# Attention and SoLU on one core: moving squares, row sums, additions and a weight combination within a quad

## The chip, the core and the metric

The kernel runs on one core of a Trainium2 chip. The metric is the device time of one execution, in microseconds (us), and lower is better. Five engines work side by side, each through its own queue in order: TensorE (PE; its weight loads are shown as PEld), VectorE (DVE), ScalarE (ACT), GpSimd (POOL) and SyncE (SP), which here issues nearly all DMAs. They meet through semaphores.

## The reference

```python
def _attn_ref(q, k, v, g_q, g_k):            # q, k, v: (8, 12, 448, 64)
    def rmsnorm(x, g):
        rms = np.sqrt(np.mean(x * x, axis=-1, keepdims=True) + 1e-06)
        return x / rms * g
    q_n, k_n = (rmsnorm(q, g_q), rmsnorm(k, g_k))
    scores = 1.0 / np.sqrt(q.shape[-1]) * np.matmul(q_n, k_n.transpose(0, 1, 3, 2))
    scores = scores - np.max(scores, axis=-1, keepdims=True)
    attn = np.exp(scores)
    attn = attn / (np.sum(attn, axis=-1, keepdims=True) + 1e-09)
    return np.matmul(attn, v).astype(np.float32)

def _moe_ref(x, w_in, w_out, g_ln):          # x: (3584, 768), w_in: (768, 1024), w_out: (1024, 768)
    h = x @ w_in
    e = np.exp(h - np.max(h, axis=-1, keepdims=True))
    sm = e / (np.sum(e, axis=-1, keepdims=True) + 1e-09)
    solu = h * sm
    mu = np.mean(solu, axis=-1, keepdims=True)
    var = np.mean((solu - mu) ** 2, axis=-1, keepdims=True)
    ln = (solu - mu) / np.sqrt(var + 1e-06) * g_ln
    return (ln @ w_out).astype(np.float32)
```

The output of the attention, reordered to (batch x sequence, heads x 64), is the x of the second part. The weights come as 64-bit floats.

## The kernel before

`fast_path` has two stages. The attention stage works on *pairs* of heads, numbered n, and on *quads* m of two pairs a = 2m and b = 2m + 1: 24 quads. The second stage, which starts when the last quad is done, multiplies by w_in and w_out in blocks of two by two with seven products each (`products`, matmuls on L953). The diff changes the attention stage alone; a slower `general_path` is compiled too and does not run here.

The order of all work in the attention stage is written out by hand (`tc.manual_schedule`): each engine runs its instructions in the order in which the Python loop over m calls the functions. `unit(f)` calls f and then what was put off with `later`.

For a pair n the steps are:

- `load(n)` (L610): eight DMAs on SyncE's queue bring q and k into `qk`. Quad m issues those of pairs 2m + 6 and 2m + 7, two of them used a quad later.
- `squares(n)` (L632): ScalarE squares `qk` into `sq`. `row_sums(n)` (L640): VectorE sums blocks of 32 into `part`. Quad m does this for quad m + 2. `fold_sums(m + 2)` (L650, L651): GpSimd joins the halves of a row of both pairs into `ss` by four copies and one addition.
- at the top of quad m, for quad m + 1: `rsqrt_seed` (L670, L671; two ScalarE instructions, into `ny`), `rsqrt_step` (L677 to L680; VectorE), and two times `normalise` (L689; GpSimd, into `qkn`).
- `qk_transpose(n)` (L699): VectorE transposes `qkn` into `qkT`; `gain(n)` (L703): ScalarE scales the half that belongs to q.
- `scores` and `scores_last` (L771, L784): TensorE, into three PSUM buffers `s`; `exponentials` (L761): ScalarE, seven a quad, into `E`.
- `add(n)` (L798): VectorE adds two tiles of E into `es`, so that `sums` (L843) needs fewer matmuls for the row sums of the softmax. In the last two quads `add_more` (L803) adds a third.
- `values_last`, `values` (L813, L824) and `sums` on TensorE; `inverse` (L854, L855 on VectorE, L862 on GpSimd) and, a unit later, `divide` (L869, L870; into `xo`), and `store_x` (L875; SyncE, to DRAM).

Beside this, the weights are turned into 32-bit floats: `load_w` brings one piece a quad into `raw` (L503 for w_in, L508 for w_out), and `convert_w` yields `low_bits` (L525, L526; ScalarE), `join` (L531, L532; VectorE) and, for w_out, `product` (L537; ScalarE), which run in three quads in turn. From quad 12 on, `combine(w_in, ...)` (L552) subtracts one block of w_in from another on GpSimd, one block a quad; quads 22 and 23 also combine two blocks of w_out. At the end of quad 22 `load_x` and `sizes` (L893, L902) begin to bring the second stage's input.

Buffers that matter here: `qk` has 4, `sq` 1, `raw` 2, and the tag `x` of the pool `xs`, 4, which the first two pairs use at the start and the second stage later.

Of the kernel before, what the change touches and what calls it, by code (L numbers as in the profile page):

```python
# [9 lines left out]
FP32 = mybir.dt.float32  # L10
U32 = mybir.dt.uint32
# [355 lines left out]
def fast_path(  # L367
# [26 lines left out]
    DM, DFF = moe_w_in.shape  # L394
# [97 lines left out]
    def load_w(step):  # L492
        src, c, i = step
        n = HO if src is moe_w_out else DFF // 2
        if second is None:
            raw = work.tile([P, DFF // 2, 2], U32, tag="raw", name="raw", bufs=2)[:, 0:n]
        else:

            raw = second.tile([P, S, 2], U32, tag="again", name="raw", bufs=2)[:, 0:n]
        w = src.bitcast(U32)[:, 2 * i * n : 2 * (i + 1) * n]  # L500
        to = raw.rearrange("p n t -> p (n t)")
        if src is moe_w_in:
            nc.sync.dma_start(to, w[c * P : (c + 1) * P])  # L503
        else:

            for g in range(4):
                r = ((c // HF * 4 + g) * HF + c % HF) * 32
                nc.sync.dma_start(to[g * 32 : g * 32 + 32], w[r : r + 32])  # L508
        return raw
# [37 lines left out]
    def combine(w, x):  # L547

        c, i = divmod(x, 4)
        b11, b21, b22, t1, t3, t2, t4 = [w[:, k, c] for k in range(7)]  # L550
        o, p, q = [(t3, b22, t1), (t1, t1, b11), (t2, b22, t1), (t4, b21, t2)][i]
        nc.gpsimd.tensor_tensor(o, p, q, OP.subtract)  # L552
# [50 lines left out]
    def load(n):  # L603
        b, hp = divmod(n, NP)
        h0 = 2 * hp
        d = st[n] = {}
        d["qk"] = loads.tile([P, 2, NB, 32], FP32, tag="qk", name="qk", bufs=4)
        for s, src in enumerate((q, k)):
            for g in range(4):
                nc.sync.dma_start(  # L610
                    d["qk"][g * 32 : g * 32 + 32, s],
                    src[b, h0 + g // 2].rearrange("(b t) (x d) -> x t b d", t=32, x=2)[g % 2],
                )
# [14 lines left out]

    def squares(n):
        d = st[n]  # L630
        d["sq"] = work.tile([P, 2 * NB, 32], FP32, tag="sq", name="sq", bufs=1)
        nc.scalar.activation(d["sq"], d["qk"].rearrange("p s b d -> p (s b) d"), AF.Square)  # L632


# [1 line left out]
    def row_sums(n):  # L636
        m, i = divmod(n, 2)
        if i == 0:
            norms[m] = {"part": small.tile([P, 2, 2 * NB], FP32, tag="part", name="part", bufs=2)}
        nc.vector.tensor_reduce(norms[m]["part"][:, i], st[n]["sq"], AX, OP.add)  # L640
# [41 lines left out]
    def normalise(n, e=nc.gpsimd):  # L682
        d = st[n]
        if ("one", n) in norms:
            y = norms["one", n]["y"]
        else:
            y = norms[n // 2]["y"][:, n % 2 * 2 * NB : (n % 2 + 1) * 2 * NB]
        d["qkn"] = work.tile([P, 2 * NB, 32], FP32, tag="qkn", name="qkn", bufs=2)
        e.tensor_tensor(  # L689
            d["qkn"],  # L690
            d["qk"].rearrange("p s b d -> p (s b) d"),
            y.rearrange("p b -> p b ()").to_broadcast([P, 2 * NB, 32]),
            OP.mult,
        )

    def qk_transpose(n):
        d = st[n]
        d["qkT"] = work.tile([P, 2, S], FP32, tag="qkT", name="qkT", bufs=3)
        nc.vector.transpose(d["qkT"].rearrange("p s t -> p (s t)"), d["qkn"].rearrange("p b d -> p (b d)"))  # L699
# [95 lines left out]
    def add(n):  # L795
        d = st[n]
        d["es"] = work.tile([P, 2, S], FP32, tag="es", name="es")
        nc.vector.tensor_tensor(d["es"], d["E", 0], d["E", 1], OP.add)  # L798
# [350 lines left out]
    with tc.manual_schedule():  # L1149
# [19 lines left out]
        for m in range(NQ):  # L1169
            a, b = 2 * m, 2 * m + 1  # L1170

            def outputs():
                values_last(m)
                values(a)


            next1 = m + 1 < NQ
            next2 = m + 2 < NQ
            next3 = m + 3 < NQ
            if m == 0:  # L1180
                unit(lambda: scores(a, 0))
                normalise_rows(1, 0)
                normalise_rows(1, 1)
                unit(lambda: scores(a, 1))
                for s in range(2):
                    transpose_rows(1, s)
                    take_rows(1, s)
                squares(2)
                row_sums(2)
                unit(lambda: scores(a, 2))  # L1190
                fold_one(2)
                unit(lambda: scores_last(m))
                rsqrt_seed(norms["one", 2])
                rsqrt_step(norms["one", 2])
                normalise(2)
                add(a)
                unit(lambda: scores(b, 0))
                unit(lambda: scores(b, 1))
                unit(lambda: scores(b, 2))
                squares(3)  # L1200
                row_sums(3)
                qk_transpose(2)
                fold_one(3)
                gain(2)
                rsqrt_seed(norms["one", 3])
                add(b)
                rsqrt_step(norms["one", 3])
                normalise(3)
                load_v(1)
                load(6)  # L1210
                load(7)
                for _ in range(2):
                    load_next()
                unit(outputs)
                squares(4)
                row_sums(4)
                unit(lambda: values(b))
                squares(5)
                unit(lambda: sums(m))
                inverse(m)  # L1220
                qk_transpose(3)
                row_sums(5)
                fold_sums(2)
                later(1, lambda m=m: divide(m))
                continue
            early = 1 < m and next1
            if early:
                rsqrt_seed(norms[m + 1])
                rsqrt_step(norms[m + 1])
                normalise(a + 2)  # L1230
                normalise(b + 2)
            if next1:
                load_v(m + 1)
            unit(lambda: scores(a, 0))
            store_x(m - 1)
            if early:
                qk_transpose(a + 2)
                if next3:
                    load(a + 6)
            unit(lambda: scores(a, 1))  # L1240
            if m == 1:
                gain(b)
            unit(lambda: scores(a, 2))
            unit(lambda: scores_last(m))
            add(a)
            unit(lambda: scores(b, 0))
            if m == 1:
                rsqrt_seed(norms[m + 1])
                rsqrt_step(norms[m + 1])
                normalise(a + 2)  # L1250
                normalise(b + 2)
                load(a + 6)
                load(b + 6)
            unit(lambda: scores(b, 1))
            if early:
                qk_transpose(b + 2)
                if next3:
                    load(b + 6)
            if m >= NQ // 2:
                combine(w_in, m - NQ // 2)  # L1260
            if m >= NQ - 2:
                for i in range(2):
                    combine(w_out, 2 * (m - NQ + 2) + i)
            unit(lambda: scores(b, 2))
            if m == 1:
                qk_transpose(a + 2)
            if next2:
                squares(a + 4)
                row_sums(a + 4)
            if next1:  # L1270
                gain(a + 2)
            add(b)
            if m == 1:
                qk_transpose(b + 2)
            if next1 and m > 1:
                gain(b + 2)
            if next2:
                squares(b + 4)
            if m == 1:
                gain(b + 2)  # L1280
            if next2:
                row_sums(b + 4)
                fold_sums(m + 2)
            add_more(a)
            add_more(b)
            unit(outputs)
            step(m - 2)
            begin(m)
            step(m - 1)
            if m - 1 in sets:  # L1290
                load_next()
            unit(lambda: values(b))
            if m == NQ - 1:
                block_sums(0, "A", 0)
                block_sums(0, "A", 1)
                load_x(1)
            unit(lambda: sums(m))
            inverse(m)
            if next1:
                later(1, lambda m=m: divide(m))  # L1300
            if m == NQ - 2:
                load_x(0)
                sizes(0)
# [105 lines left out]
```

## Time and profile before

| | |
|---|---|
| median of three runs | 852.91 us (852.55 to 857.69) |
| the profiled execution | 855.39 us, of which the profile's span is 853.6 us |
| granted TensorE clock, mean | 0.998 |
| PE, DVE, ACT, POOL busy in the span | 830.1, 616.3, 375.9, 323.1 us |
| attention stage | up to 342.3 us of the span |
| squares L632 (ACT), 46 | 972 ns each |
| row sums L640 (DVE), 46 | 1074 ns each |
| fold's copies L650 (POOL), 88 | 374 ns each |
| normalisations L689 (POOL), 46 | 1713 ns each |
| transposes L699 (DVE), 46 | 1101 ns each |
| additions L798 (DVE), 48 | 1350 ns each |
| combinations of w_in L552 (POOL), 12 | 1271 ns each |

The span runs from the first to the last instruction of the profiled execution; all positions in it are counted from its start. A row of the timeline has a start, a length, the engine, the line, the operation, what is written and read, and a count where like instructions are merged; a bracket at its end tells how long the engine had been idle and what ended that. "SPq" rows are SyncE issuing DMAs. A matmul's end is modelled, so that a busy TensorE may still be waiting; the distance between the same instruction of two quads is the better measure.

### The profile page before, as it was taken

The page shows a single profiled execution, that of the slowest core. Times are in us where ns is not written, and L with a number is a line of the kernel's source. Part 1 is how long each engine was busy: PE and PEld are TensorE (multiplying, and loading weights), DVE is VectorE, ACT ScalarE, POOL GpSimd, SP SyncE. Part 2 cuts the span into 40 slices and gives each one's busy share as a digit, 9 for nine tenths or more (in the row PEclk, how much of TensorE's full clock was granted, in tenths as well). Part 3 has the DMA queues.
Part 4 walks back from the last instruction along what each step waited for, and adds up shares of the span by engine and source line. Part 5 has one row for each costly group of instructions (what it writes and reads, how often), then busy time and mean ns, then how long its engine had stood idle before and what let it go on. Part 6 is the DMA issues. An engine that isn't in the chain of part 4 may idle for free.

```text
span 853.6 us, 13057 instructions
## 1 busy us (share of the span) xinstructions
PE 830.1 (97%) x4432; PEld 481.6 (56%) x4432; DVE 616.3 (72%) x990; ACT 375.9 (44%) x559; POOL 323.1 (38%) x464
## 2 busy tenths in 40 slices
PE   5999999999999999999999999999999999999997
PEld 2334434333433333444444444445999999999996
DVE  5778988799998889589999999999933333333322
ACT  5677877778787776155445453443200000000000
POOL 1444443546455457222333223554333222233220
PEclk9999999999999999999999999999999999999999
DMA  5677777888767673234443444453564445544331
GB/s 119 138 173 177 171 178 156 181 188 172 175 146 174 135 188 118 73 97 132 109 124 105 128 113 105 135 137 92 153 227 151 151 151 182 179 151 141 119 117 41
DMA packets 268060, 121.63 MB, mean 142 GB/s; under 512 B 190672, under 2 KB 250064, under 8 KB 267984
## 3 DMA queue, kind: packets, MB, share of 16 engines
q1 hardware_dynamic: 253584, 110.65, 50.4%
q10 hardware_dynamic: 14400, 10.06, 4.1%
q8 instruction: 37, 0.61, 0.3%
q14 instruction: 39, 0.32, 0.1%
HBM read 83.96 MB, written 36.70 MB: 141 GB/s over the span
## 4 chain that ended last, share of the span: by engine, by line
PE 67%; DVE 11%; SPq 7%; DMA 7%; ACT 3%; issue 2%; POOL 2%; ACTq 0%; POOLq 0%; DVEq 0%
PE b L953 59%; SPq L610 7%; DVE es L798 3%; PE o L824 3%; PE s L771 2%; DVE qkT L699 2%; DVE part L640 2%; DMA v<-in_v_dram 1%; POOL ss L650 1%; DVE r L869 1%; ACT E L761 1%; DMA qk<-in_k_dram 1%; PE sm L843 1%; DMA raw<-in_moe_w_in_dram 1%; DVE xo L870 1%
## 5 line engine op out<-in xcount | busy, mean ns | idle before, releaser
L953 PE MATMUL b<-w_out,uT 128*128 128x384 f32 x448 | 151.4, 486 | 0.0
L953 PE MATMUL b<-w_in,xg 128*128 128x512 f32 x336 | 151.1, 592 | 0.0
L953 PEld LDWEIGHTS b<-w_out,uT 128*128 128x128 f32 x448 | 138.1, 308 | 6.7 <-issue 0.2
L761 ACT ACTIVATE E<-s 128x896 f32<-128x896 f32 x168 | 138.8, 931 | 4.2 <-PE s L771 3.3
L771 PE MATMUL s<-qkT 64*64 64x448 f32 x1152 | 127.1, 567 | 0.8 <-DVE qkT L754 0.8
L966 ACT COPY q<-b 128x512 f32<-128x512 f32 (+1 forms) x28 | 14.9, 532 | 251.7 <-PE b L953 239.0
L953 PE MATMUL b<-w_out,us 128*128 128x384 f32 x336 | 115.4, 486 | 0.0
L953 PE MATMUL b<-w_in,xsum 128*128 128x512 f32 x252 | 115.0, 592 | 0.0
L824 PE MATMUL o<-E,v 128*64 128x448 f32 x576 | 113.5, 543 | 0.0
L953 PEld LDWEIGHTS b<-w_in,xg 128*128 128x128 f32 x336 | 63.8, 190 | 80.2 <-issue 78.3
L953 PEld LDWEIGHTS b<-w_out,us 128*128 128x128 f32 x336 | 103.5, 308 | 4.8
L689 POOL TENSOR_TENSOR qkn<-qk,ny 128x896 f32<-128x896 f32 x46 | 77.9, 1713 | 31.2 <-DVE ny L680 10.8
L771 PEld LDWEIGHTS s<-qkT 64*64 64x64 f32 x1152 | 45.6, 166 | 67.6 <-ACT E L761 35.7
L953 PEld LDWEIGHTS b<-w_in,xsum 128*128 128x128 f32 x252 | 47.9, 190 | 60.3 <-issue 58.4
L650 POOL COPY ss<-part 32x56 f32<-32x56 f32 x88 | 32.9, 374 | 125.5 <-DVE part L640 122.7
L824 PEld LDWEIGHTS o<-E,v 128*64 128x64 f32 x576 | 39.2, 137 | 72.7 <-issue 61.4
L1033 POOL TENSOR_TENSOR he<-he,mhalf 128x1 f32<-128x1 f32 x28 | 17.6, 630 | 160.1 <-DVE he L1032 159.8
L933 POOL TENSOR_TENSOR us<-uT 128x512 f32<-128x512 f32 x14 | 17.8, 1272 | 149.9 <-DMA uT<-ud 108.9
L962 DVE TENSOR_TENSOR y<-b,u 128x384 f32<-128x384 f32 x42 | 23.4, 557 | 62.0 <-PE b L953 62.0
L798 DVE TENSOR_TENSOR es<-E 128x896 f32<-128x896 f32 x48 | 64.7, 1350 | 0.0
L1039 ACT ACTIVATE u<-u,shift,he 128x1024 f32<-128x1024 f32 x28 | 34.6, 1237 | 63.3 <-POOL shift L1035 63.3
L640 DVE TENSOR_REDUCE part<-sq 128x28 f32<-128x896 f32 x46 | 49.4, 1074 | 13.6 <-ACT sq L632 12.9
(106 smaller groups left out, 1056.5 us busy)
## 6 DMA issues: line engine op xcount, KB each, us to landing
ud<-ub SPq DMA_DIRECT2D x112, 128.0 KB, 2.5
uT<-ud SPq DMA_DIRECT2D x56, 256.0 KB, 4.3
xd<-xo SPq DMA_DIRECT2D x24, 448.0 KB, 3.8
out_dram<-y SPq DMA_DIRECT2D x27, 384.0 KB, 2.6
qk<-in_q_dram SPq DMA_DIRECT2D x184, 56.0 KB, 2.7
qk<-in_k_dram SPq DMA_DIRECT2D x184, 56.0 KB, 2.3
v<-in_v_dram SPq DMA_DIRECT2D x24, 384.0 KB, 5.0
raw<-in_moe_w_in_dram SPq DMA_DIRECT2D x12, 512.0 KB, 4.6
```

The source lines that it names most:

```text
L610: nc.sync.dma_start(d["qk"][g * 32 : g * 32 + 32, s], src[b, h0 + g // 2].rearrange("(b t) (x d) -> x t b d", t=32, x=2)[g % 2],)
L640: nc.vector.tensor_reduce(norms[m]["part"][:, i], st[n]["sq"], AX, OP.add)
L650: e.tensor_copy(ss[g * 32 : g * 32 + 32], part[o * 32 : o * 32 + 32])
L689: e.tensor_tensor(d["qkn"], d["qk"].rearrange("p s b d -> p (s b) d"), y.rearrange("p b -> p b ()").to_broadcast([P, 2 * NB, 32]), OP.mult,)
L761: nc.scalar.activation(d["E", kc], s[:, :, 0:S], AF.Exp)
L771: nc.tensor.matmul(s[c : c + D, h, 0:S], d["qkT"][hh, 1, keys], d["qkT"][hh, 0, :], start=True, stop=True,)
L798: nc.vector.tensor_tensor(d["es"], d["E", 0], d["E", 1], OP.add)
L824: nc.tensor.matmul(d["o"][h * D : (h + 1) * D, :], quads[n // 2]["v"][:, n % 2 * 2 + h, kc], d["E", kc][:, h], start=False, stop=(kc == NJ ...
L933: nc.gpsimd.tensor_tensor(s1, a21, a22, OP.add)
L953: nc.tensor.matmul(o, a[:, c] if kind == "A" else a[:, :, c], w[:, i, c], start=(c == 0), stop=(c == last))
L962: nc.vector.tensor_tensor(out, k["o"], k[x], OP.add)
L1039: nc.scalar.activation(d["u"], d["u"], AF.Identity, scale=d["e"], bias=d["shift"])
```

## The change

In the loop over quads:

- From quad 5 on (`scarce` is false) both pairs' `squares` stand first, then both `row_sums` (with the gains between them on ScalarE), then GpSimd's `fold_sums`, and only then the second addition, `add(b)`. In quads 1 to 4 the order around `add(b)` changes slightly.
- From quad 2 on the first addition, `add(a)`, is called after `scores(b, 1)` and so follows both transposes on VectorE, where it had stood between them.
- `combine(w_in, ...)` is called right behind the two `normalise` at the top of the quad.

And three buffers: `sq` has 2 in place of 1, `qk` 5 in place of 4, and `raw` takes slots of the tag `x` in place of 2 of its own.

VectorE's order in a quad from 5 on, before: `qkT`, `es`, `qkT`, `part`, `es`, `part`, joins; after: `qkT`, `qkT`, `es`, `part`, `part`, `es`, joins. ScalarE's, before: `sq`, two gains, `sq`; after: two `sq`, two gains. The order of the instructions on TensorE, GpSimd and SyncE is the same in both; the waits of SyncE's `raw` loads for ScalarE and VectorE are gone.

```diff
-            raw = work.tile([P, DFF // 2, 2], U32, tag="raw", name="raw", bufs=2)[:, 0:n]
+            raw = xs.tile([P, DFF // 2, 2], U32, tag="x", name="raw")[:, 0:n]
...
-        d["qk"] = loads.tile([P, 2, NB, 32], FP32, tag="qk", name="qk", bufs=4)
+        d["qk"] = loads.tile([P, 2, NB, 32], FP32, tag="qk", name="qk", bufs=5)
...
-        d["sq"] = work.tile([P, 2 * NB, 32], FP32, tag="sq", name="sq", bufs=1)
+        d["sq"] = work.tile([P, 2 * NB, 32], FP32, tag="sq", name="sq", bufs=2)
...
                 normalise(a + 2)
                 normalise(b + 2)
+            if m >= NQ // 2:
+                combine(w_in, m - NQ // 2)
...
             unit(lambda: scores(a, 2))
             unit(lambda: scores_last(m))
-            add(a)
+            if m < 2:
+                add(a)
             unit(lambda: scores(b, 0))
...
-            if m >= NQ // 2:
-                combine(w_in, m - NQ // 2)
+            if m > 1:
+                add(a)
             if m >= NQ - 2:
                 for i in range(2):
                     combine(w_out, 2 * (m - NQ + 2) + i)
             unit(lambda: scores(b, 2))
             if m == 1:
                 qk_transpose(a + 2)
+            scarce = m < 5
             if next2:
                 squares(a + 4)
+                if not scarce:
+                    squares(b + 4)
                 row_sums(a + 4)
             if next1:
                 gain(a + 2)
-            add(b)
             if m == 1:
+                add(b)
                 qk_transpose(b + 2)
-            if next1 and m > 1:
+            if next1:
                 gain(b + 2)
-            if next2:
+            if scarce:
                 squares(b + 4)
-            if m == 1:
-                gain(b + 2)
+                if m > 1:
+                    add(b)
             if next2:
                 row_sums(b + 4)
                 fold_sums(m + 2)
+            if not scarce:
+                add(b)
```

## The prediction

> **What bounds the kernel now.** I read the page first: shares of busy time, then the chain that ended last.
>
> ```profile
> PE 830.1 (97%) x4432; PEld 481.6 (56%) x4432; DVE 616.3 (72%) x990; ACT 375.9 (44%) x559; POOL 323.1 (38%) x464
> ...
> PE 67%; DVE 11%; SPq 7%; DMA 7%; ACT 3%; issue 2%; POOL 2%; ACTq 0%; POOLq 0%; DVEq 0%
> ```
>
> TensorE is the bound, but the second line holds 11% VectorE and 7% SyncE. The merged chain puts all of that before 342.41 us, in the attention stage; from there TensorE runs without a break for 497.65 us, in lines that the diff does not touch. So only the 24 quads count. From the first `sums` matmul (L843) of a quad to that of the next the PE rows give 12.90 us in quads 5 and 6 (the program's m), 13.50 in 13 to 15, 13.23 in 16 to 18, then 14.09, 14.74, 14.66. At 12.90 throughout, quads 7 to 23 would save 12.4 us: 1.5%, the most that any reordering here can bring. Busy time by stretch (after the length: PE, PEld, DVE, ACT, POOL):
>
> ```profile
> 190.00:259.00 69.00, 68.48 (x680) 26.91 (x680) 63.95 (x94) 54.68 (x80) 36.82 (x62) 1.00 0.76 172
> 259.00:313.00 54.00, 50.97 (x480) 19.07 (x472) 46.07 (x70) 41.16 (x60) 27.73 (x47) 1.00 0.71 152
> ```
>
> In the first, VectorE works 63.95 of 69 us (93%); in the second only 85%, and still the quads are longer. Something else rules there. First the timeline of quad 14:
>
> ```profile
> 211.96 1.27 POOL L552 TENSOR_TENSOR w_in<-w_in 128x512 f32<-128x512 f32 x1
> 212.00 2.17 DVE L798 TENSOR_TENSOR es<-E 128x896 f32<-128x896 f32 x1
> ...
> 216.09 1.07 DVE L798 TENSOR_TENSOR es<-E 128x896 f32<-128x896 f32 x1
> ...
> 217.18 1.09 DVE L640 TENSOR_REDUCE part<-sq 128x28 f32<-128x896 f32 x1
> ```
>
> The same addition takes 2.17 us beside GpSimd's subtraction and 1.07 alone: it stands still until 213.23 and then runs for 0.95. One of the two waits for the other's whole instruction. Now SyncE's own rows (start, length, DMAs issued):
>
> ```profile
> 301.31 0.53 SPq L875 DMA_DIRECT2D xd<-xo  x1
> 301.95 2.23 SPq L610 DMA_DIRECT2D qk<-in_q_dram  x4
> 304.22 2.06 SPq L610 DMA_DIRECT2D qk<-in_k_dram  x4
> 306.39 2.77 SPq L610 DMA_DIRECT2D qk<-in_q_dram  x4
> 309.21 2.04 SPq L610 DMA_DIRECT2D qk<-in_k_dram  x4
> ```
>
> Each group begins where the last one ended. It is so from 57 us to 313 us: the semaphore rows ahead of the loads of `qk`, `raw` and `v` last 0.02 to 0.03 us, so their buffers are free long before; what lengthens an issue is the landing of earlier DMAs, or a row of 1.2 to 2.0 us once a quad. A quad's issues (16 of `qk` at 0.52, 3 of `v`, 1 of `xd`, 1 to 4 of `raw`) took (301.95 - 43.03) / 19 = 13.6 us, and 14.4 to 14.7 in the last three, more than TensorE's 12.90. SyncE starts with a lead and loses it; from quad 18 the second square starts 0.3 us after its load has landed, four quads running. The chain at the last such load:
>
> ```profile
> 310.77 2.12 DMA qk<-in_k_dram
> ...
> 313.20 0.96 ACT sq L632
> ```
>
> So the attention stage ends a fixed stretch after SyncE's last `qk` load lands, at 312.90. That stretch, from the timeline:
>
> ```profile
> 314.18 1.09 DVE L640 TENSOR_REDUCE part<-sq 128x28 f32<-128x896 f32 x1 [0.34 <-ACT sq L632]
> ...
> 317.03 0.30 POOL L651 TENSOR_TENSOR ss<-ss,part 128x56 f32<-128x56 f32 x1
> ...
> 317.89 5.75 ACT L761 ACTIVATE E<-s 128x896 f32<-128x896 f32 x7
> ```
>
> Second row sums, GpSimd's fold, two ScalarE instructions for the seed, then the next quad's exponentials. TensorE's scores follow these at 0.82 us each, so what the first exponential loses, TensorE loses.
>
> **The change, part by part.**
>
> *The first addition behind both transposes; w_in's combination.* GpSimd's order of instructions does not change: the combination already followed the two normalisations in its queue. What changes is VectorE: the second `qkT` now covers the 1.27 us, and the addition follows at 1.07. (The first `qkT` of quad 14 took its usual 1.10 beside GpSimd's normalisation, so the second should not wait.) Worth 1.1 us of VectorE in quads 12 to 21.
>
> *Both squares and row sums first (quads 5 to 21).* The second square no longer waits for the first row sum (0.30 us idle) and stands ahead of two gains (0.65 each). In quad 14 (first square at 213.24 for 0.95 us, second at 216.20) it could start at 214.2, but by the trace its load lands at 214.91. Over all quads from 5, square minus landing was 0.2 to 3.2 us before, 0.7 to 1.9 in quads 13 to 17: the order removes that slack and no more. No load comes earlier for it. The gains behind it end at landing + 1.9 and + 2.6 (0.3 + 0.95 + 0.65 each); the next quad's scores start at landing + 3.2 (316.09 less 312.90) and use the first of them: nothing, TensorE's `sums` (2.0 us) hide it, with 1.3 us of cover.
>
> *The fold ahead of the second addition.* On VectorE the addition now follows the row sum directly, ahead of the two joins (L531, L532; 0.55 each with w_out, 0.68 with w_in). GpSimd's first copy starts 0.2 us after the row sum. Before, it met the joins: the four copies took 1.54 us (two at 0.42 to 0.55, two at 0.23), so they already wait on VectorE instructions with two SBUF operands. Now the first copy meets an addition (about 1.0), the second and third the joins, and only the last is free: 1.0 + 0.55 + 0.55 + 0.3 = 2.4 after the row sum against 1.7 before, 0.7 late, and the seed with it. That no row shows this pair makes bounds: 0 if the copies pass first, +1.0 if all of the addition is added. I take +0.75, nearest to the GpSimd subtractions in quad 23, which take 1.85 us between additions and 0.99 without. The addition itself is late for `sums` by at most 1.1 us (ends at landing + 3.4), but TensorE would then wait for the exponentials anyway (landing + 5.0 before, 5.75 after). In quads with a late load this 0.75 does not add up: the next load's landing sets the next quad. It is paid once, after the last.
>
> *Quad 22.* No squares. Before, the first addition met w_in's subtraction, and the two of w_out hid partly behind the second transpose; after, four additions (0.97) and two subtractions (1.1) take turns: 1.03 + 1.03 + 3.9 + 2.2 = 8.2 us against 7.85 (321.36 to 329.21). +0.3; bounds -0.4 (TensorE's own wait there is 0.41) to +0.35.
>
> *Buffers.* A fifth `qk`, a second `sq`, `raw` in the four slots of `x`. The program drops SyncE's wait ahead of 18 `raw` loads: 0.06 us each, so -1.0 if every one counts, 0 if the landings swallow it; I take -0.4. The waits themselves were met anyway, so the fifth buffer starts nothing sooner.
>
> Sum: +0.75 + 0.3 - 0.4 = +0.65 us on the span of 853.6, in an execution of 855.39 (1.8 lie around the span). The median of the runs is 852.91, so the forecast is 853.6; its own bounds are -1.4 to +1.35, so 851.5 to 854.3 before the spread of the runs (852.55 to 857.69).
>
> The Trainium skill ("Perfetto Trace Analysis", Identifying the Most-Contended Engine) says to look for the engine with the highest occupancy and judges VectorE by it. By that rule VectorE's 93% is the bound from 190 to 259 us and its 1.1 us should come back as time, as in the first rival; the rows of SyncE speak against it.
>
> **Rivals.** *VectorE is the bound.* For it: 93%, and a chain from 184 to 257 us that runs through `qkT`, `es`, `part` and names no SyncE row. Then quads 12 to 18 fall to 12.90: 0.51 + 0.60 + 0.61 + 0.59 + 3 x 0.33 = 3.3 us saved, 849.6. Against: SyncE would have to be early, and second squares there start 0.7 to 3.2 us after landing. *The loads come sooner too* (the fifth buffer or the freed `raw` counts): quads 10, 11, 19, 20, 21 add 1.34 + 1.51 + 1.19 + 1.84 + 1.76 = 7.6; 10.9 in all, 842.0. Against: the 0.03 us waits. *Slower: the fold's wait is paid in every quad.* One mechanism: the copies held behind the second addition, 0.75 us, in quads 5 to 21; it decides from the point where a quad's period hangs on the fold alone and not on SyncE, as quads 12 to 17 nearly do. All 17 give +12.8: 865.7; only quads 12 to 17 give +4.5: 857.4. Against: where the load is early, the fold starts up to 2.0 us sooner and pays for it. *It does nothing*: no queue but VectorE's and ScalarE's is reordered; within 0.3 us of before, inside the forecast's bounds.
>
> **How the numbers follow.** Forecast (with the case of nothing) 0.80, first rival 0.07, loads sooner 0.04, slower 0.09, a third of that at the full price. The range, 847.5 to 858.5, holds the forecast with the spread of runs, the first rival with 2 us of spread below it, and the small slower case. 1% is 8.5 us, about what a measurement of this kernel can tell from no change: faster by more needs the loads (0.04), slower by more the full price (0.03); within, 0.93.
>
> **What would show it.** Right: mean of the `es` additions of quads 12 to 21 near 1.1 (total of L798 down by some 11 us); second squares idle on a `qk` load in most quads from 5; the four copies (L650) longer; the last `qk` load landing at 312 to 314; TensorE entering the second stage at 342 to 344. Wrong: quads 19 to 21 well under 14 us, a last landing before 310, or quads of even 12.90 us.

## The result and the profile after

The changed kernel takes 853.92 us in the median of 12 executions (851.99 to 857.85), the kernel before on the same chip 855.21 us (851.13 to 858.83). The ratio is 1.000, 95% interval 0.9976 to 1.0024: no difference that shows. The forecast was 853.6 us and no change. The profiled execution of after took 853.61 us, its span is 851.8 us.

The page, shares of busy time and the chain that ended last:

```profile
PE 827.4 (97%) x4432; PEld 482.5 (57%) x4432; DVE 605.8 (71%) x990; ACT 373.9 (44%) x559; POOL 335.1 (39%) x464
...
PE 70%; SPq 15%; issue 4%; DMA 3%; DVE 3%; POOL 2%; ACT 2%; ACTq 0%; POOLq 0%; DVEq 0%
```

VectorE's share of the chain fell from 11% to 3% and SyncE's rose from 7% to 15%. Busy time by stretch (after the length: PE, PEld, DVE, ACT, POOL):

```profile
190.00:259.00 69.00, 68.86 (x696) 28.27 (x688) 58.45 (x96) 53.68 (x80) 41.72 (x67) 1.00 0.74 166
259.00:313.00 54.00, 50.71 (x476) 18.85 (x476) 42.00 (x66) 40.65 (x60) 28.13 (x39) 1.00 0.69 148
```

VectorE went from 63.95 to 58.45 us in the first stretch, and from 46.07 to 42.00 in the second. Two groups of the page tell what changed, the additions on VectorE (1350 ns each before) and the fold's copies on GpSimd (374 ns):

```profile
L798 DVE TENSOR_TENSOR es<-E 128x896 f32<-128x896 f32 x48 | 53.8, 1125 | 0.0
L650 POOL COPY ss<-part 32x56 f32<-32x56 f32 x88 | 46.0, 522 | 109.4 <-DVE part L640 106.6
```

Quad 14 in the timeline. Transposes, both squares and both row sums now stand as pairs; the second transpose covers GpSimd's subtraction, and the addition takes 1.05 us in place of 2.17:

```profile
208.78 2.10 DVE L699 STREAM_TRANSPOSE qkT<-qkn 128x896 f32<-128x896 f32 x2
209.58 1.28 POOL L552 TENSOR_TENSOR w_in<-w_in 128x512 f32<-128x512 f32 x1
...
210.80 1.05 DVE L798 TENSOR_TENSOR es<-E 128x896 f32<-128x896 f32 x1
...
211.98 2.08 DVE L640 TENSOR_REDUCE part<-sq 128x28 f32<-128x896 f32 x2
```

SyncE's rows ahead of the last loads of `qk`, still without a gap, some 3 us earlier than before:

```profile
298.90 2.31 SPq L610 DMA_DIRECT2D qk<-in_q_dram  x4
301.25 2.04 SPq L610 DMA_DIRECT2D qk<-in_k_dram  x4
303.40 3.46 SPq L610 DMA_DIRECT2D qk<-in_q_dram  x4
306.91 2.05 SPq L610 DMA_DIRECT2D qk<-in_k_dram  x4
```

And the stretch behind the last load, which lands at 310.68, in the timeline. The bracket says that the square had waited 2.12 us for that load:

```profile
310.91 0.95 ACT L632 ACTIVATE sq<-qk 128x896 f32<-128x896 f32 x1 [2.12 <-DMA qk<-in_k_dram]
...
312.89 1.08 DVE L798 TENSOR_TENSOR es<-E 128x896 f32<-128x896 f32 x1
...
313.11 2.31 POOL L650 COPY ss<-part 32x56 f32<-32x56 f32 x4 [5.33 <-DVE part L640]
...
315.50 0.30 POOL L651 TENSOR_TENSOR ss<-ss,part 128x56 f32<-128x56 f32 x1
...
316.37 5.75 ACT L761 ACTIVATE E<-s 128x896 f32<-128x896 f32 x7
```

The same four copies before:

```profile
315.40 1.54 POOL L650 COPY ss<-part 32x56 f32<-32x56 f32 x4 [5.50 <-DVE part L640]
```

The four copies take 2.31 us beside the addition and the joins, 1.54 before; the exponentials follow the landing by 5.69 us, 4.99 before.

Where the attention stage's time lies, from the distance between the first `sums` matmul (L843) of one quad and of another, in us: "up to quad 4" is the position of that matmul in quad 4, "quads 5-11" the distance from there to quad 11's. All kernels of the experiments below are in the table but the four with v moved or a w_out load merged; each row is one profiled execution.

| kernel | up to quad 4 | quads 5-11 | 12-16 | 17-21 | 22 | last `qk` landing | from there to quad 23's `sums` |
|---|---|---|---|---|---|---|---|
| before | 83.14 | 93.84 | 67.13 | 69.95 | 13.56 | 312.90 | 27.75 |
| after | 85.28 | 91.16 | 64.82 | 70.68 | 14.15 | 310.68 | 28.26 |
| after, once more | 83.95 | 92.11 | 64.48 | 71.01 | 14.01 | 310.15 | 28.27 |
| after, two more DMAs a quad | 85.09 | 97.23 | 71.38 | 76.59 | 14.86 | 329.73 | 28.27 |
| before + buffers | 84.11 | 90.27 | 66.11 | 68.17 | 14.14 | 308.14 | 27.70 |
| before + first addition | 83.55 | 92.84 | 67.75 | 70.30 | 14.30 | 314.01 | 27.58 |
| before + both | 83.42 | 91.90 | 68.41 | 70.12 | 14.23 | 313.43 | 27.51 |
| before, w_out load of 128 rows in a row | 84.54 | 90.54 | 68.88 | 66.15 | 13.24 | 306.68 | 29.71 |
| after, w_out load of 128 rows in a row | 84.19 | 91.00 | 65.20 | 64.49 | 12.89 | 297.22 | 33.35 |
| after, store from GpSimd | 85.11 | 90.28 | 64.48 | 64.48 | 12.90 | 299.98 | 30.06 |

Five quads of 12.90 are 64.5. In the last three rows the last landing comes too early to set the end. From before to after, profile against profile, the stage ends 1.71 us sooner: +2.14 up to quad 4, -2.68, -2.31, +0.73, +0.59 and -0.18 in quad 23. Executions of the kernel before lay between 850.0 and 861.7 us over all chips, so one profile does not make an effect; what repeats between profiles is used below.

### The profile page after: what moved, and what is told of

It reads as the page before. It is cut to its first block, busy times and chain, and to the rows that moved or that the text cites. A ratio compares the mean times of both kernels' runs of the same rounds, so it can differ in the third digit from the quotient of the medians.

```text
span 851.8 us, 13064 instructions
## 1 busy us (share of the span) xinstructions
PE 827.4 (97%) x4432; PEld 482.5 (57%) x4432; DVE 605.8 (71%) x990; ACT 373.9 (44%) x559; POOL 335.1 (39%) x464
## 4 chain that ended last, share of the span: by engine, by line
PE 70%; SPq 15%; issue 4%; DMA 3%; DVE 3%; POOL 2%; ACT 2%; ACTq 0%; POOLq 0%; DVEq 0%
PE b L953 59%; SPq L610 12%; PE s L771 4%; PE o L824 4%; DMA qk<-in_k_dram 2%; POOL ss L650 2%; PE sm L843 1%; SPq L627 1%; ACT sq L632 1%; SPq L508 1%; DVE part L640 1%; DMA v<-in_v_dram 1%; PE s L784 1%; DVE es L798 1%; PE o L813 1%
## 5 line engine op out<-in xcount | busy, mean ns | idle before, releaser
L771 PE MATMUL s<-qkT 64*64 64x448 f32 x1152 | 124.3, 559 | 1.4 <-ACT xsq L724 0.8
L650 POOL COPY ss<-part 32x56 f32<-32x56 f32 x88 | 46.0, 522 | 109.4 <-DVE part L640 106.6
L771 PEld LDWEIGHTS s<-qkT 64*64 64x64 f32 x1152 | 46.2, 165 | 64.5 <-ACT E L761 33.1
L1048 DVE STREAM_TRANSPOSE ub<-u 128x1024 f32<-128x1024 f32 x28 | 57.3, 2053 | 0.0
```

The source lines that it names most:

```text
L650: e.tensor_copy(ss[g * 32 : g * 32 + 32], part[o * 32 : o * 32 + 32])
L771: nc.tensor.matmul(s[c : c + D, h, 0:S], d["qkT"][hh, 1, keys], d["qkT"][hh, 0, :], start=True, stop=True,)
L1048: nc.vector.transpose(ub.rearrange("p b i c -> p b c i"), mt.pop(t)["u"].rearrange("p (b c j) -> p b c j", c=HF, j=32))
```

## Experiments

**The same kernel once more.** No edit, one execution.

> The changed kernel itself once more, for its profile: how far the quads of one execution differ from another's. Theory 1: quads 7 to 15 at 12.90 again, the last qk load at 309 to 314 us, quads 17 to 21 over 13.4. If the even quads of 12.90 were an accident of one execution, they are gone here.

853.55 us. Quads 12 to 15 at 12.90 came again, and quads 17 to 21 took 13.9 to 14.7 (13.5 to 14.7 in the first). Quads 7 to 11 were not all even: quad 7 took 14.34, 13.65 in the first, and two more 13.0 to 13.1. The gain in the middle and its end in the late quads are seen in both profiled executions.

**Is it SyncE that paces? Two more small DMAs a quad.**

```diff
+    def more(m):
+        for i in range(2):
+            t = small.tile([32, 32], FP32, tag="more", name="more", bufs=4)
+            nc.sync.dma_start(t, q[0, 0, 32 * i : 32 * i + 32, 0:32])
...
             store_x(m - 1)
+            more(m)
```

> The changed kernel with two more small DMAs (4 KB each, into a tile that nothing reads) on SyncE's queue in each quad from 1 on, behind the store of xo: some 0.95 us of issue more a quad, 20 quads up to the last qk load. Theory 1: the last qk load lands 10 to 20 us later and the time grows by as much (864 to 874). Rival A and every theory in which the loads have room: less than 3 us.

874.43 us, ratio to before 1.0218 (1.0175 to 1.0262), by the ratio 18.7 us more. TensorE, VectorE, ScalarE and GpSimd got no work, and quads 17 to 21 grew by 5.9 us, 1.2 a quad. No VectorE bound does that. Quads 5 to 16, most of them at 12.90 in after, grew by 12.6 us: SyncE had no room there either.

**Taking v off SyncE's queue.** The loads of v and vl issued from ScalarE behind the quad's last exponentials, in both kernels:

```diff
-            if next1:
-                load_v(m + 1)
             unit(lambda: scores(a, 0))
...
             unit(lambda: scores(b, 2))
+            if next1:
+                load_v(m + 1, nc.scalar)
```

> The changed kernel, with the three v loads of a quad issued by ScalarE behind the quad's last exponentials instead of by SyncE (about 1.75 us of issue a quad less on SyncE). Theory 1 (SyncE's issues pace the attention stage once its lead is gone, and the change only pays where the loads are early): the last qk load lands some 15 us or more earlier relative to the quad that uses it, quads 16 to 21 fall from 13.2 to 14.7 us to about 12.9, and the time falls by 8 to 12 us against the kernel before (842 to 846 for 853 to 855). Rival A (the transfers themselves, not the issues, are the limit): less than 2 us. Rival B (the change has no effect on the compute of a quad): as fast as the same edit on the kernel before.

> The kernel before with the same edit. Theory 1: the quads that waited for loads (10, 11, 19 to 21) fall to 12.9 to 13.5, but quads 12 to 21 stay at 13.2 to 13.5, VectorE's own sum with its addition behind GpSimd's subtraction; 4 to 8 us less than before, and 3 to 5 us slower than the changed kernel with the edit. Rival A: less than 2 us. Rival B: equal to the changed kernel with the edit.

A miss of 50 us: 897.57 us, ratio 1.0476 (1.0443 to 1.0509), and 909.55, ratio 1.0651 (1.0603 to 1.0699). The waits of SyncE's queue in the first (who waited for whom, total us, times, longest) show why:

```profile
SPq L610 <- DMA v<-in_v_dram: 58.5, 12, 7.4
...
SPq L875 <- DMA v<-in_v_dram: 37.1, 8, 6.6
```

SyncE's later loads and stores waited for landings of v, which it no longer issued; after's own list has one such wait, of 0.3 us. In the trace ScalarE's loads of v and SyncE's DMAs raise the same eight completion semaphores in turn, so a DMA moved to another engine's queue still held SyncE. That the changed kernel was 12 us the faster here is told, but not counted: neither kernel keeps its loads in time.

**Fewer issues for w_out.** Four DMAs of 32 rows become one of four times 32 rows:

```diff
-            for g in range(4):
-                r = ((c // HF * 4 + g) * HF + c % HF) * 32
-                nc.sync.dma_start(to[g * 32 : g * 32 + 32], w[r : r + 32])
+            rows = w.rearrange("(h g c j) x -> h c g j x", g=4, c=HF, j=32)
+            nc.sync.dma_start(to, rows[c // HF][c % HF])
```

> The changed kernel with each 32-row quarter of a w_out load taken by one DMA instead of four (same bytes, same place, three issues fewer in each of quads 13 to 20; the output is complete). Theory 1 (SyncE's issues set the late quads): 3 issues of 0.46 us are 1.4 us of a quad, so quads 17 to 21 fall from 13.5 to 14.7 us to between 12.9 and 13.4, the last qk load lands at 302 to 306 instead of 310.7, and the span falls by 4 to 7 us, to 845 to 848. Rival A (issue time goes by the pieces of a DMA and not by their number, or the DMA engines and not SyncE are late): the one issue lasts some 1.7 us, quads 17 to 21 stay at 13.5 to 14.7, span 851 to 853. Rival B (VectorE, with the two joins of w_out in these quads, is the bound there): loads land early, but quads 17 to 21 stay above 13.8, span above 850.

> The kernel before with the same edit: each w_out load by one DMA. Theory 1: quads 19 to 21 fall from 14.1 to 14.7 us to the 13.2 to 13.5 that VectorE's order leaves there, so 3 to 5 us are saved (span 849 to 851), quads 10 and 11 stay above 14, quads 12 to 18 stay at 13.2 to 13.5, and the changed kernel with this edit is the faster of the two by 3 to 5 us: the change's gain in VectorE shows in the end once the loads come in time. Rival A: no change within 1 us. Rival B: quads 19 to 21 stay above 14 with loads that land early.

Another miss: 882.52 us, ratio 1.0284 (1.0248 to 1.0319), and 879.94, ratio 1.0270 (1.0235 to 1.0305); quads 16 to 22 took 14.7 to 20.7 us. SyncE's rows of the first, one quad:

```profile
229.53 0.58 SPq L507 DMA_DIRECT2D raw<-in_moe_w_out_dram  x1
...
232.69 5.88 SPq L609 DMA_DIRECT2D qk<-in_q_dram  x4
238.87 2.35 SPq L609 DMA_DIRECT2D qk<-in_k_dram  x4
```

The one issue is short (0.58 us), so the first half of rival A is out. But the load lands at 237.83, 8.3 us after its issue, where the four landed after 2.2 to 3.7 each, and the issue that begins at 237.84 is the eighth behind it (v, two of vl, `xd`, four of `qk`): it waited for that landing, and the next, at 238.87, for v's at 238.86. But these two waits are 0.3 us each. Most of the 5.88 us is the issue ahead of them, 3.11 us long (234.47 to 237.57), and the DMA eight ahead of that one had landed at 231.04; what holds an issue so long while the slow load is under way is not shown. So SyncE's pace is made of 0.5 us an issue, of waits for the eighth-last landing, and of issues that last longer for another reason. The Trainium skill ("DMA: Bandwidth & Descriptors", Why a DMA increments its semaphore by 16 and not by 1) says that a DMA runs on as many engines, up to 16, as divide the slowest dimension of both sides, which for an outer dimension of 4 would be four engines; the trace agrees: this load's semaphore is raised in one step at 230.54 and four from 237.46 to 237.83, where a `qk` load's is raised in sixteen, and of the sixteen of the v load behind it twelve come by 234.71 and the last four from 238.30 to 238.86. That the four engines are why it lands so late fits this; it was not tried by itself.

**The pieces of the change.** Buffers alone (the first three hunks), the first addition with w_in's combination alone, and both, on the kernel before.

> The kernel before with the change's buffers alone (five qk, two sq, raw in the four slots of x), its order untouched. Theory (SyncE's semaphore rows at raw cost it, and its long issue falls elsewhere): the stalls of quads 10 and 11 go (14.2 and 14.4 to about 13), quads 12 to 18 stay at 13.2 to 13.5 because the first addition still takes 2.1 us, n = 47 lands at 309 to 312; span 852 to 853.5. Rival (buffers are worth nothing, as the prediction held): quads as before within 0.3 us each, 14.2 to 14.4 in 10 and 11, landing at 312 to 314, span 853 to 854.

> The kernel before with the first addition behind both transposes and w_in's combination behind the normalisation, and nothing else of the change (the squares, the fold and the buffers as before). Theory (in quads 12 to 18 VectorE was the bound after all): first additions near 1.1 us and quads 12 to 16 fall from 13.2 to 13.5 to 12.9 to 13.1; quads 10 and 11 stay at 14.2 to 14.4; the gain of some 2 us is given back in quads 17 to 21, whose loads land no earlier; span within 1 us of 853.6. Rival (the gain of the middle quads comes from the buffers and SyncE): quads 12 to 18 stay at 13.2 to 13.5 though the additions are short. Rival (the gain lasts): span 850 to 851.

> The kernel before with the buffers and with the first addition behind both transposes (and w_in's combination behind the normalisation), but with its old order of squares, gains, fold and second addition: what the two single pieces, run before, give together. Theory (two limits that take turns: buffers relieve SyncE, the addition VectorE): quads 12 to 16 at 12.9 (64.5 to 65.0 together, against 66.1 with the buffers alone and 67.8 with the addition alone), quads 17 to 21 still 68 to 71, attention within 1.5 us of the changed kernel's, so the order of squares and fold counts for nothing. Rival (squares first is what frees the middle quads): quads 12 to 16 above 65.5. Rival (the fold ahead of the addition costs in the late quads, 0.75 us each): quads 17 to 21 here 3 us or more below the changed kernel's 70.7 to 71.0, span 847 to 849.

855.12 us, ratio 0.9985 (0.9963 to 1.0006); 855.42, ratio 0.9993 (0.9968 to 1.0019); 855.39, ratio 1.0002 (0.9973 to 1.0030). None differs from before in time.

In the traces the first addition does what was said: 1.11 us in the mean of quads 12 to 21 with the piece, 2.16 without. It brings nothing by itself: quads 12 to 16 67.75 against 67.13. With the buffers alone quads 7 to 12 took 12.90 and quads 13 to 18 13.1 to 13.4, as the theory had it. But both together, which should have given 64.5, gave 68.41: its loads were late from quad 9 on (squares idle on a `qk` load 21.0 us in all, 6.1 in before). That expectation failed. Each piece has one profile, and they are not alike: that of the buffers alone (850.54 us) was the fastest of its twelve executions, that of both (856.17 us) one of the slower, where three of twelve took 849.9 to 850.2. What the profiles have in common is where SyncE's one long issue of a quad (1 to 2 us) falls. One quad of before + both, and one of after:

```profile
161.47 3.03 SPq L610 DMA_DIRECT2D qk<-in_q_dram  x4
164.87 2.32 SPq L610 DMA_DIRECT2D qk<-in_k_dram  x4
167.29 1.98 SPq L610 DMA_DIRECT2D qk<-in_q_dram  x4
169.31 3.32 SPq L610 DMA_DIRECT2D qk<-in_k_dram  x4
...
173.68 1.26 SPq L627 DMA_DIRECT2D vl<-in_v_dram  x2
```

```profile
148.79 2.41 SPq L610 DMA_DIRECT2D qk<-in_q_dram  x4
151.24 2.04 SPq L610 DMA_DIRECT2D qk<-in_k_dram  x4
153.39 1.98 SPq L610 DMA_DIRECT2D qk<-in_q_dram  x4
155.41 2.05 SPq L610 DMA_DIRECT2D qk<-in_k_dram  x4
...
158.51 2.29 SPq L627 DMA_DIRECT2D vl<-in_v_dram  x2
```

In the first it falls on the last `qk` group, and the first group of the quad is longer as well (3.03 against an undisturbed 1.98): 14.2 us from one `xd` to the next. In the second it falls on vl, and the first group takes 2.41: 12.75. Over the eight profiles of the table without added DMAs or a moved store, quads that start between 94 and 196 us: 12.92 us in the mean where the longest issue is of raw, v or vl (39 quads), 13.66 where it is of `qk` (24 quads), though single quads overlap (12.2 to 13.7 and 12.0 to 15.0). In the two profiles of after 15 of 16 such quads are of the first kind, in before 2 of 8, with the buffers alone 7 of 8, with both pieces 4 of 8. The long issue comes with an instruction packet: in these profiles, from 94 to 310 us, 126 of the 128 packets of 16 KB on the instruction queue overlap an issue of 0.85 us or more, and 121 of the 133 issues over 1 us overlap one. So what differs is where SyncE stands in its order when the packet comes. Which kind an execution falls into is not the order of VectorE alone, and with one profile a piece and no run that moved the packets it stays open what decides it, and whether the packet is the cause of the long issue.

**SyncE relieved.** Each w_out load of the attention stage as one DMA of 128 rows that follow each other. This leaves out the order of w_out's rows, so the second stage does the same work on other values and the output is not the reference's:

```diff
+            if second is None:
+                nc.sync.dma_start(to, w[c * P : (c + 1) * P])
+                return raw
             for g in range(4):
```

> The changed kernel with each w_out load of the attention stage as one DMA of 128 rows in a row, in the form of the w_in loads, which keep SyncE in step in quads 8 to 15; the rows of w_out then stand in another order, so what the second stage computes is not the reference's, with the same work. Theory 1 (SyncE paces the late quads: 3 more issues of 0.46 us): quads 17 to 21 fall from 70.7 us together to 65 to 67 (12.9 to 13.4 each), n = 47 lands at 304 to 307, span 846 to 848. Rival A (VectorE and GpSimd with the joins of w_out set these quads): 70 to 71 us as before, n = 47 landed 3 us or more ahead of its square. Rival B (a DMA of this size lands so late that it holds the eighth issue behind it, as where the four were one strided DMA, there 8.5 us): quads 17 to 21 above 14.5, span above 853.

> The kernel before with each w_out load of the attention stage as one DMA of 128 rows in a row (the rows of w_out in another order, so the second stage does the same work on other values), as it was run with the changed kernel, whose quads 17 to 22 then took 12.9 us each and its executions 846.84 us in the median. Theory (the change takes 1.1 us from VectorE, which counts where SyncE is early): the loads come in time here too, but quads 13 to 21 stay at 13.1 to 13.5 us with first additions of 2.1 us and squares that wait for VectorE and not for loads, so 2 to 4 us of the gain are missing: median 849 to 851.5, ratio to the kernel before 0.993 to 0.996, and the changed kernel with this edit is the faster of the two by 2 to 4 us. Rival A (VectorE is no bound either: the addition's 1.1 us lay beside other work): quads 13 to 21 at 12.9, median within 1 us of 846.8. Rival B (SyncE still loses its lead, through the old buffers): quads 10 and 11 above 14 and quads 17 to 21 above 13.8, median 852 to 855.

846.84 us, ratio 0.9921 (0.9896 to 0.9946), for the changed kernel: 7 us below its own 853.92 on another chip. Quads 16 to 22 take 12.90 us each. That is more than expected (64.5 us in quads 17 to 21, not 65 to 67): n = 47 lands at 297.2, and its square starts 4.3 us later, behind other work of ScalarE. 851.64 us, ratio 0.9939 (0.9912 to 0.9965), for the kernel before, just outside the 849 to 851.5 expected, since quads 13 to 15 (14.1, 13.9, 14.4) still waited for loads. Its quads 16 to 22 take 13.23 us each, with first additions of 2.17 us and the loads 2 to 6 us ahead of their squares; its chain from 222 to 300 us runs mostly through VectorE (additions 21%, transposes 16%, row sums 11%). The chain of the changed kernel and, from both, the windows from 259 to 300 us, changed kernel first:

```profile
PE 91%; DVE 4%; SPq 2%; issue 1%; DMA 1%; POOL 1%; ACT 1%; POOLq 0%; ACTq 0%; DVEq 0%
```

```profile
259.00:300.00 41.00, 41.00 (x412) 17.29 (x408) 35.66 (x58) 34.79 (x52) 25.89 (x39) 1.00 0.80 185
```

```profile
259.00:300.00 41.00, 41.00 (x404) 16.10 (x400) 37.78 (x58) 33.01 (x49) 22.20 (x41) 1.00 0.76 169
```

In the same 41 us TensorE issued 412 matmuls after and 404 before: PE reads as busy in both, and the counts tell the difference. VectorE is at 87% and 92%. So with loads in time the change is worth 0.33 us a quad. Rivals A and B fall for the changed kernel, rival A for the kernel before, and of rival B only quads 13 to 15 are left. Of the times, the medians differ by 4.8 us, but on two chips, and the ratios by 0.0018 with intervals that overlap, so the 2 to 4 us expected are shown by the quads and not by the times.

**A complete kernel on this road: the store from GpSimd.** In `store_x`, `nc.sync.dma_start` becomes `nc.gpsimd.dma_start`.

> The changed kernel with the store of xd (one a quad) issued from GpSimd in place of SyncE; the output is complete. Theory 1: one issue of 0.55 us a quad less on SyncE is worth 0.55 us in each quad that SyncE sets: 17 to 21 and two or three of quads 1 to 4, so 3 to 4 us: quads 17 to 21 together 67.5 to 68.5, span 848 to 849.5. Rival A (as with v on ScalarE: DMAs of another engine hold SyncE's later issues): quads of 14 us and more all along, span above 860. Rival B (GpSimd pays: the issue or the wait for xo stands in its queue ahead of the normalisation): qkT later, quads above 13.2 from quad 2 on, span 853 to 860.

851.91 us, ratio 0.9959 (0.9922 to 0.9996): the best version that computes everything, by little. The store costs GpSimd 0.76 us a quad:

```profile
L875 POOL DMA_DIRECT2D xd<-xo x24 | 18.1, 756 | 6.0 <-DVE xo L870 6.0
```

In the profiled execution (844.93 us) all quads from 4 on take 12.90 us, which is more than one issue of 0.55 us in the late quads was expected to give. Four of the twelve executions lay under 847 us and six above 852; the trace shows one of the former, and that SyncE loses its lead in the others is likely but not shown. The Trainium skill ("Perfetto Trace Analysis", DMA Optimizations) says that DMAs may be balanced over the engines that can issue them, or inputs parted from outputs. Here the output alone on GpSimd gained 0.4%, and v on ScalarE lost 4.8% and 6.5%.

## Why the prediction was right, and where not

*The bound: right.* SyncE's issues set the late quads: two more a quad cost 18.7 us, three fewer in the quads of w_out gave 7. The chain of after, with 15% SyncE and 3% VectorE, says the same. The stage still ends a fixed stretch after the last landing: 28.26, 28.27 and 28.27 us in three profiles of the changed order, 27.5 to 27.75 in four of the old one, over landings from 308 to 330 us.

*The fold: right in mechanism, place and size.* Predicted +0.75 once, with copies of 2.4 us in place of 1.7 after the row sum and exponentials at landing + 5.75. Measured: copies of 2.31 in place of 1.54, exponentials at landing + 5.69, +0.70. In quads whose load is early it costs nothing: 12.90 us with the fold behind the addition.

*The slower rival* priced this 0.75 us in each of quads 5 to 21. The quads of 12.90 rule it out.

*The first addition: right in size, half right in worth.* L798 fell by 10.9 us, some 11 were said. The prediction gave it no worth in time, because of SyncE. That holds in quads 17 to 21. In quads 12 to 16 the first rival was nearer: after runs them in 64.8 and 64.5 us, where the kernel before and its variants read 66.1 to 68.9, and with loads in time before stays at 13.23 a quad where after runs 12.90. Of that rival's 3.3 us, 2.6 lay in quads 12 to 16, and in the two profiles of after 2.3 and 2.65 came. Then 0.7 and 1.1 us went back in quads 17 to 21, since a quad that ends sooner waits longer for the next load: second squares stand idle for loads in quads 15 to 21, 1.2 to 2.7 us each.

*Squares first, and "no load comes earlier": wrong.* Squares idle on a load in most quads from 5 on was said; in after there are 11 such waits, seven of them in quads 15 to 21, and none in 7 to 14. The loads did come earlier: n = 46's first issue at 298.90 and 298.43 (301.95 before), the last landing at 310.68 and 310.15, where 312 to 314 was predicted, and TensorE enters the second stage at 340.6 and 340.1, not at 342 to 344. The step that failed is the one that took SyncE's 13.6 us a quad as given. In quads that start from 94 to 196 us it was 12.9 or 13.7 in the mean, by where its long issue falls, and in after it fell well through quads 8 to 15; that this is what makes the difference is read from the profiles and was not tried. Of the prediction's own signs of being wrong one came true, quads of even 12.90 us. Quads 10 and 11, 14.24 and 14.41 before and left as they are by the prediction, ran at 12.90.

*Quad 22: the sign was wrong, within its bounds.* +0.3 was taken (-0.4 to +0.35). Comparing the stretch behind the last landing with and without the moved addition, in the old order of the fold: 27.58 against 27.75, and 27.51 against 27.70, so -0.2. The fold is then 28.27 - 27.55 = +0.7, as above. The -0.2 shows between quad 22's `sums` and quad 23's. The distance up to quad 22's, 14.15 against 13.56, is mostly the fold's, since the load was late in both; with loads in time it is 12.89.

*The buffers: not told apart.* -0.4 was taken; the ratio with the buffers alone leaves anything from -3.2 to +0.5 us. Of SyncE's semaphore rows ahead of `raw` loads 16 went, not 18.

*Not foreseen:* up to quad 4 after was 0.8 to 2.1 us later than before. Over all rows of the table the changed order reads 84.0 to 85.3 there and the old one 83.1 to 84.5, which overlap; no run was made for it, and it stays open.

So the sum: stretch +0.51 (+1.05 said), landing -2.22 (-0.4 said), the rest -0.07, together -1.78 on the profiled executions, +0.65 said. The ratio's interval is 2 us wide to either side, so the times can't tell these two sums apart: "no change" is right, and that it came out right with the landing missed by 1.8 us is in part luck. The forecast did not know of the 5.0 us (4.4 in the second profile) that quads 5 to 16 gain. What it did know, the late quads bound by SyncE and the fold behind the last landing, took back 0.7 to 1.1 and 0.7 us of it, the later start up to quad 4 another 2.1 and 0.8, and 1.7 to 2.2 us were left in the profiles.

## What to carry to other kernels

Where two resources are near the same pace, the one with no lead decides: find the queue whose rows have no gap, and do to it what costs nothing elsewhere, one issue more or less, before the order of a busy engine is changed. A gain in a middle stretch is worth what is left of it at the last landing, so follow a fixed stretch back from the end and compare landings, not busy shares. Merging or moving DMAs is measured by their landing and by who waits for it, not by the issues saved.

## What the runs showed of the hardware

DMAs of the same bytes took 8.3 us to land as four groups of 32 rows in one, 2.2 to 3.7 us each as four; as one of 128 rows in a row, 3.3 to 4.6 us, and in the changed kernel the quads from 16 on took 12.90 us. An issue of SyncE waited for the landing of the eighth DMA ahead of it (begun at 237.84, landed at 237.83). Nearly each quad has one SyncE issue of 1 to 2 us instead of 0.5, and it coincides with a packet of 16 KB on the instruction queue (126 of 128 packets); whether the packet is the cause wasn't tried. And the additions and GpSimd's work take turns: with the fold beside the addition a copy of 0.23 us took 0.95, and an addition of 1.07 us took 2.17 beside a subtraction of 1.27.
